# Sparse attention with a soft mixture of experts on one core: halving steps for the key chunks' minimum and maximum, the head product on GpSimd, and another order of the steps

## The chip, the core and the metric

The kernel runs on one core of a Trainium2 chip. A core has five engines that run side by side, each working through its own list of instructions in order: TensorE (PE in the profile; its weight loads are PEld), VectorE (DVE), ScalarE (ACT), GpSimd (POOL) and SyncE (SP). They wait for one another through semaphores. [...] Data comes from HBM through 16 DMA engines. In this kernel GpSimd issues all loads and SyncE issues all stores. The metric is the device time in microseconds, the median of three runs.

## What is computed

The first half is attention over chosen chunks of keys: 4 batches, 8 heads, 768 positions, head size 64. For each query and each chunk of 32 keys an upper bound of the score is made from the chunk's elementwise minimum and maximum, and the six best chunks (among those not in the future) take part in the attention.

```python
k_min = np.min(k_chunks, axis=3); k_max = np.max(k_chunks, axis=3)
ub = np.sum(np.maximum(q[:, :, :, None, :] * k_min[:, :, None, :, :],
                       q[:, :, :, None, :] * k_max[:, :, None, :, :]), axis=-1)
ub = np.where(causal, ub, -1e9)
top_chunks = np.argsort(ub, axis=-1)[..., -6:]
scores = np.where(sel & causal_mask, q @ k.T / 8, -1e9)
out = softmax(scores) @ v
```

The second half takes the 3072 rows of 512 that come out (x) through a soft mixture of 8 experts with 4 slots each: `logits = x @ phi`; a softmax down the rows gives each slot's input `d.T @ x`; each expert is `relu(slot @ w1) @ w2`; and a softmax over the slots spreads the results back to the rows, `c @ slot_out`.

## The kernel before

**Tiling.** Two heads make a pair, and 16 pairs (four to a batch) pass through a software pipeline: the loop at L469 runs over i, and one turn works on several pairs at once. It computes the scores of pair i, multiplies with the values for pair i-1, normalises and transposes the result of pair i-2, chooses chunks for pair i+1 and prepares keys and queries of pair i+2. "Pair i" in the text means turn i.

**Steps for a pair.** `load` (L122) issues the key and query loads on GpSimd's queue, four pairs ahead; `load_v` and `load_w` issue values and expert weights there too. `transposes` (L177) and `evac_T` (L189) bring keys and queries to SBUF as `kT` and `qT`, head size down the partitions, the copy on ScalarE. `kmin` and `kmax` (L199 to L213) reduce 24 chunks of 32 keys on VectorE into `mm`; then a product with `headsel` makes `bd`, in which each head's numbers stand in its own columns. `qsplit` (L215) splits queries into negative and positive part, `qpn`. `ubound` (L223) is 18 matmuls that make the bounds of all chunks, the causal term among them. `select` (L238) finds the eight largest per row with 12 instructions (`mx`), writes one column through a cast on GpSimd, and marks the chunks that are not chosen (`ns_t`). `ns_transposes` and `evac_ns` turn these marks into `nsT`. `scores(i, g)` (L264) makes one of six groups of score blocks: products of `kT` and `qT`, then a second pair of matmuls that add the mask from `nsT` and `smask`. `expo` (L283) is the exponential on ScalarE and, on GpSimd, the causal cut of the diagonal blocks. `pv` (L297) multiplies with the values. `normalise` (L313) divides (`inv`, `x_sb`), `x_transposes` and `evac_x` give `xT`.

**Steps for a batch.** When the last pair of a batch is through, the mixture's steps run inside the loop: `moe_logits`, `moe_copy` (`lg` and the row maximum `pm`), `moe_max` and `moe_bound` (the maximum over rows, `mb`), `moe_exp` (its spread `bc`, the running maximum `m_run`, the shifted logits `ld`, their exponential `d_sb`, the factor `dm`, and the rescaling of `si_acc`), `moe_comb` (`rm`, `lc`, and two exponentials into `c_pad`), `moe_dispatch` (`si_ps`) and `moe_ct` (`cT_all`). All of it falls in turn i-2 (logits and copy) and turn i-3 (the rest), counted from the batch's last pair. Batch 3 has its steps after the loop, before the experts.

**What sets the order.** The program is under a manual schedule: each engine gets its instructions in the order in which the Python code writes them. Nothing is moved by a planner. So a step that is written later on one engine waits behind everything that was written before it there.

**Buffers that tie engines together.** Score tiles come from `p_sc` with two buffers, so group g+2 needs the exponential of group g to be done. Transposes, bounds, marks and the mixture's small products share `p_tp` with two buffers (tag "tp"): each allocation needs the tile of the second allocation before it to have been read out. Exponentials are kept in nine buffers. Key and query inputs have three buffers each. Weights of the 16 expert matrices are loaded one a turn by a plan, in turns 2, 5, 8 and 11 none, in turns 12 and 13 two.

Of the kernel before, what the change touches and what calls it, by code (L numbers as in the profile page):

```python
# [46 lines left out]
def kernel(  # L47
# [61 lines left out]
    tpu = u_ctx.enter_context(tc.tile_pool(name="tpu", bufs=2, side="right"))  # L109
    inp = l_ctx.enter_context(tc.tile_pool(name="inp", bufs=3, side="right"))  # L110
# [87 lines left out]

    def kmin(i):  # L199
        kT = st["kT", i].rearrange("d (c x) -> d c x", x=CH)  # L200
        mm = tpu.tile([P, 2, 1, NCHUNK], BF16, name="mm", tag="mm")
        nc.vector.tensor_reduce(mm[:, 0, 0, :], kT, axis=AX.X, op=ALU.min)  # L202
        st["mm", i] = mm

    def kmax(i):
        kT = st["kT", i].rearrange("d (c x) -> d c x", x=CH)
        mm = st.pop(("mm", i))
        nc.vector.tensor_reduce(mm[:, 1, 0, :], kT, axis=AX.X, op=ALU.max)  # L208
        bd = tpu.tile([P, 2, 2, NCHUNK], BF16, name="bd", tag="bd")
        nc.vector.tensor_tensor(  # L210
# [144 lines left out]
    def moe_copy(b):  # L355
        lg = small.tile([P, NQT, NS], F32, name="lg", tag="lg")
        pm = small.tile([P, NS], F32, name="pm", tag="pm")
        ps = st.pop(("lgps", b))
        if b == B - 1:
            nc.vector.tensor_reduce(pm, ps.rearrange("p t s -> p s t"), axis=AX.X, op=ALU.max)  # L360
            nc.scalar.copy(lg, ps)
        else:
            nc.vector.tensor_copy(lg, ps)
            nc.vector.tensor_reduce(pm, lg.rearrange("p t s -> p s t"), axis=AX.X, op=ALU.max)
        st["lg", b], st["pm", b] = lg, pm
# [14 lines left out]
    def moe_exp(b):  # L380
        lg = st["lg", b]
# [3 lines left out]
        )  # L385
        m_new, m_old = m_run[b % 2], m_run[(b + 1) % 2]
# [51 lines left out]
    def moe_ct(b):  # L438
# [5 lines left out]
        nc.vector.tensor_copy(cT_all[:, b * NQT:(b + 1) * NQT, :], ps)  # L444
# [24 lines left out]
    for i in range(-2, NPAIR):  # L469
# [238 lines left out]
```

## Time and profile before

| | |
|---|---|
| median of three runs | 177.93 us (177.87 to 177.99) |
| the profiled execution's own time | 177.53 us |
| its span, first to last instruction | 175.8 us |
| TensorE, VectorE, ScalarE, GpSimd busy | 139.1, 128.8, 120.0, 99.9 us |
| first exponential of pairs 0, 1, 5, 9, 13 | 15.60, 23.48, 52.06, 82.47, 113.82 us |
| first exponential of pairs 14 and 15, end of the last one | 121.00, 130.21, 135.68 us |
| mean granted TensorE clock | 0.95 |

Times within the profile count from the first instruction. The profiled execution took 1.7 us more than its span, which lies around it. A busy share is an average over the start, the 16 turns and the tail (experts and output, from 144 us on), which have different limits. In a line of a timeline, the first number is the start, the second the time from the first to the last of the instructions merged into it, then engine, line, operation, the tile written and the tiles read, shapes and count; a bracket at the end gives the engine's idle time before it and what ended it. The lines of the changed kernel have other numbers, so groups are named by their tiles.

### The profile page before, as it was taken

What the parts mean: (1) busy time and instruction counts of PE and PEld (TensorE: products, weight loads), DVE (VectorE), ACT (ScalarE), POOL (GpSimd) and SP (SyncE); (2) the same over time, 40 slices, a digit from 0 to 9 for tenths busy, and PEclk for the clock granted to TensorE, in tenths of its full rate; (3) what the DMA queues carried; (4) which work ended last, traced back from release to release, by engine and by line L of the source; (5) the groups of instructions that cost most, each with busy time, mean ns of one, the idle gap of its engine ahead of it and who ended that gap; (6) DMA issues with size and microseconds to landing.
All of it is one profiled execution on the core that took longest, in us unless ns stands there. A gap on an engine that the chain in (4) does not pass through costs nothing.

```text
span 175.8 us, 5994 instructions
## 1 busy us (share of the span) xinstructions
PE 139.1 (79%) x2486; PEld 95.9 (55%) x2486; DVE 128.8 (73%) x429; ACT 120.0 (68%) x163; POOL 99.9 (57%) x194
## 2 busy tenths in 40 slices
PE   0449888999889889999988999999689569986500
PEld 0334556777567657766765776677467444532000
DVE  4456979999889998999998999999752650246530
ACT  2336798989789778988977698897667321156430
POOL 7995679869768557877775585759344600000000
PEclk9999999999999999999999999999999956999755
DMA  3999999999999999999999999199999993009995
GB/s 50 167 158 180 194 206 200 206 197 209 179 212 193 215 185 143 200 172 203 172 147 203 169 207 141 17 187 211 200 214 214 213 215 72 4 13 403 402 405 212
DMA packets 40460, 32.92 MB, mean 187 GB/s; under 512 B 26353, under 2 KB 34545, under 8 KB 40433
## 3 DMA queue, kind: packets, MB, share of 16 engines
q0 software_dynamic: 38416, 26.25, 101.8%
q1 hardware_dynamic: 2016, 6.29, 9.1%
q8 instruction: 19, 0.31, 0.7%
q14 instruction: 9, 0.07, 0.1%
HBM read 52.49 MB, written 6.29 MB: 334 GB/s over the span
## 4 chain that ended last, share of the span: by engine, by line
PE 36%; ACT 19%; DVE 13%; DMA 12%; POOL 11%; issue 5%; POOLq 0%; DVEq 0%; ACTq 0%
ACT e_sb L289 13%; DMA k_in<-in_k_dram 7%; PE sc_ps L271 6%; DMA out_dram<-o_sb 5%; PE at_ps L308 5%; PE sc_ps L277 4%; PE tr_ps L184 3%; PE h_ps L605 3%; DVE x_sb L321 3%; POOL e_sb L291 3%; POOL q_in L127 2%; PE ns_ps L253 2%; POOL k_in L127 2%; PE so_ps L640 2%; PE si_ps L427 2%
## 5 line engine op out<-in xcount | busy, mean ns | idle before, releaser
L289 ACT ACTIVATE e_sb<-sc_ps 128x1024 bf16<-128x1024 f32 x96 | 83.6, 936 | 10.9 <-PE sc_ps L277 9.9
L291 POOL TENSOR_SCALAR_AFFINE_SELECT e_sb<-e_sb 128x256 bf16<-128x256 bf16 x96 | 39.5, 423 | 32.7 <-ACT e_sb L289 32.0
L271 PE MATMUL sc_ps<-qT,kT 64*128 64x512 bf16 (+3 forms) x256 | 39.6, 310 | 6.6 <-ACT e_sb L289 6.3
L277 PE MATMUL sc_ps<-nsT,smask 64*128 64x512 bf16 (+3 forms) x256 | 36.8, 306 | 0.0
L308 PE MATMUL at_ps<-v_t,e_sb 128*128 128x65 bf16 x672 | 29.4, 194 | 1.2 <-DVE x_sb L321 1.1
L308 PEld LDWEIGHTS <-e_sb 128*128 128x128 bf16 x672 | 25.1, 98 | 3.4 <-DVE x_sb L321 1.6
L271 PEld LDWEIGHTS <-kT 64*128 64x128 bf16 x256 | 15.8, 94 | 16.8 <-issue 8.7
L242 DVE MAX8 mx<-ub_ps 128x8 f32<-128x24 f32 x192 | 18.8, 170 | 4.6 <-PE ub_ps L231 4.5
L202 DVE TENSOR_REDUCE mm<-kT 128x24 bf16<-128x768 bf16 x16 | 15.2, 949 | 4.0 <-ACT kT L193 4.0
L132 POOL DMA_DIRECT2D v_t<-in_v_dram x16 | 16.7, 1042 | 1.9 <-PE ns_ps L253 1.2
L193 ACT COPY kT<-tr_ps 128x768 bf16<-128x768 bf16 x16 | 12.8, 803 | 6.5 <-PE tr_ps L184 6.5
L321 DVE TENSOR_TENSOR x_sb<-at_ps,inv 128x768 bf16<-128x768 f32 (+2 forms) x17 | 15.5, 910 | 0.6
L277 PEld LDWEIGHTS <-smask 64*128 64x128 bf16 x256 | 13.1, 95 | 4.4 <-issue 0.3
L208 DVE TENSOR_REDUCE mm<-kT 128x24 bf16<-128x768 bf16 x16 | 15.1, 942 | 0.0
L193 ACT COPY qT<-tr_ps 128x768 bf16<-128x768 bf16 x16 | 13.2, 825 | 2.7 <-PE tr_ps L184 2.7
L184 PE MATMUL tr_ps<-ident,k_in 128*64 128x128 bf16 x192 | 9.2, 237 | 6.6 <-DMA k_in<-in_k_dram 5.5
L670 DVE TENSOR_SCALAR o_sb<-o_ps,cinv 128x512 f32<-128x512 f32 x12 | 8.6, 748 | 7.2 <-PE o_ps L668 4.1
L231 PE MATMUL ub_ps<-bd,qpn 128*128 128x48 bf16 x192 | 10.4, 187 | 2.8 <-DVE qpn L218 2.5
L127 POOL DMA_DIRECT2D k_in<-in_k_dram x16 | 11.7, 729 | 1.3 <-POOLq L692 0.8
L261 DVE COPY nsT<-ns_ps 128x768 bf16<-128x768 bf16 x16 | 8.9, 556 | 4.0 <-PE ns_ps L253 3.5
L672 ACT ACTIVATE o_sb<-o_ps,cinv 128x512 f32<-128x512 f32 x12 | 7.8, 688 | 5.7 <-DMA out_dram<-o_sb 3.8
L127 POOL DMA_DIRECT2D q_in<-in_q_dram x16 | 11.5, 721 | 0.0
(95 smaller groups left out, 213.2 us busy)
## 6 DMA issues: line engine op xcount, KB each, us to landing
w_sb<-in_moe_w_dram POOLq DMA_DIRECT2D x16, 1024.0 KB, 12.9
out_dram<-o_sb SPq DMA_DIRECT2D x10, 512.0 KB, 5.5
k_in<-in_k_dram POOLq DMA_DIRECT2D x16, 192.0 KB, 7.9
q_in<-in_q_dram POOLq DMA_DIRECT2D x16, 192.0 KB, 8.1
v_t<-in_v_dram POOLq DMA_DIRECT2D x16, 192.0 KB, 9.3
out_dram<-o_sb SPq DMA_DIRECT2D x4, 256.0 KB, 3.4
phi_sb<-in_moe_phi_dram POOLq DMA_DIRECT2D x1, 32.0 KB, 9.6
```

Of the source, the lines that this page charges most:

```text
L127: nc.gpsimd.dma_start(out=t, in_=src.rearrange("h (p g) d -> p h (g d)", p=P))
L132: nc.gpsimd.dma_start(out=v_t[i % NV][:, :, :, :D], in_=v[b, 2 * j:2 * j + 2].rearrange("h (g p) d -> p h g d", p=P),)
L193: nc.scalar.copy(t.rearrange("d (p g) -> d p g", g=NQT), st.pop((nm + "ps", i)).rearrange("d g p -> d p g"),)
L202: nc.vector.tensor_reduce(mm[:, 0, 0, :], kT, axis=AX.X, op=ALU.min)
L208: nc.vector.tensor_reduce(mm[:, 1, 0, :], kT, axis=AX.X, op=ALU.max)
L242: nc.vector.max(mx[:, a, :], ub[:, a, :])
L271: nc.tensor.matmul(ps[:, h, c:c + w], lhsT=kT[r, kg * P:(kg + 1) * P], rhs=qT[r, qs], start=True, stop=False,)
L277: nc.tensor.matmul(ps[:, h, c:c + w], lhsT=smask[r, kg].rearrange("p a b -> p (a b)"), rhs=nsT[r, qs], start=False, stop=True,)
L289: nc.scalar.activation(e[:, :, :w], st.pop(("scps", i, g))[:, :, :w], func=ACT.Exp, scale=scale)
L291: nc.gpsimd.affine_select(out=e[:, :, :P], in_=e[:, :, :P], compare_op=ALU.is_ge, fill=0.0, base=0, pattern=[[0, 2], [1, P]], channel_mult ...
L308: nc.tensor.matmul(o, lhsT=st["e", i, g][:, h, c:c + P], rhs=v_t[i % NV][:, h, kg, :], start=(kg == 0), stop=(kg == t),)
L321: nc.vector.tensor_tensor(st["x", b][:, t0:t1, 2 * j:2 * j + 2, :].rearrange("p t h d -> p h t d"), at[:, :, :, :D], inv.broadcast_to([P, ...
```

## The change

The change has two parts.

First, each of the two reductions over 32 keys becomes three steps, in a new function `fold`: the two halves of 16 keys are compared elementwise, then the two halves of 8 of the result, and what is left, 8 per chunk, is reduced. The intermediate tiles lie in a new pool `tpf` with one buffer each. The product that makes `bd` moves from VectorE to GpSimd.

Second, the order of the loop changes. `qsplit` goes from the end of the turn before to behind `normalise`. The bound and the selection go behind the key transposes and the first `pv` (in the first two turns they stay in front). The key and query loads follow the selection, as before. The query transposes and their copy go from before group 4 to between groups 4 and 5, and `kmax` with them. The mixture's functions are cut into smaller ones, and a batch's steps now spread over the turns i-2 (logits), i-3 (copy, maximum, bound, the shifted logits for the combine weights, spread), i-4 (shift, exponential, rescale, weights, dispatch, the transposes of the weights) and i-5 (their copy out). After the loop the steps of batch 3 have the same order as before; the copy of batch 2's transposed weights falls there too, on ScalarE.

```diff
+    tpf = u_ctx.enter_context(tc.tile_pool(name="tpf", bufs=1, side="right"))
...
+    def fold(out, kT, op):
+        a = tpf.tile([P, NCHUNK, CH // 2], BF16, name="fold_a", tag="fold_a")
+        nc.vector.tensor_tensor(a, kT[:, :, :CH // 2], kT[:, :, CH // 2:], op=op)
+        b = tpf.tile([P, NCHUNK, CH // 4], BF16, name="fold_b", tag="fold_b")
+        nc.vector.tensor_tensor(b, a[:, :, :CH // 4], a[:, :, CH // 4:], op=op)
+        nc.vector.tensor_reduce(out, b, axis=AX.X, op=op)
+
     def kmin(i):
...
-        nc.vector.tensor_reduce(mm[:, 0, 0, :], kT, axis=AX.X, op=ALU.min)
+        fold(mm[:, 0, 0, :], kT, ALU.min)
...
     def kmax(i):
...
-        nc.vector.tensor_reduce(mm[:, 1, 0, :], kT, axis=AX.X, op=ALU.max)
+        fold(mm[:, 1, 0, :], kT, ALU.max)
         bd = tpu.tile([P, 2, 2, NCHUNK], BF16, name="bd", tag="bd")
-        nc.vector.tensor_tensor(
+        nc.gpsimd.tensor_tensor(
             bd, mm.broadcast_to([P, 2, 2, NCHUNK]), headsel.broadcast_to([P, 2, 2, NCHUNK]), op=ALU.mult,
         )
...
-        moe(moe_max, i - 3)
-        if have(i + 1):
-            ubound(i + 1)
         if have(i - 2):
             normalise(i - 2)
-        moe(moe_bound, i - 3)
+        moe(moe_copy, i - 3)
+        moe(moe_shift, i - 4)
+        moe(moe_exp, i - 4)
+        moe(evac_ct, i - 5)
         if have(i + 1):
+            qsplit(i + 1)
+        if i <= 0 and have(i + 1):
+            ubound(i + 1)
             select(i + 1)
         if have(i + 2):
             transposes(i + 2, "k")
             evac_T(i + 2, "k")
+        if have(i - 1):
+            pv(i - 1, [0, 1, 2])
+        if i > 0 and have(i + 1):
+            ubound(i + 1)
+            select(i + 1)
         if i == -1:
             ns_transposes(0)
             evac_ns(0)
         if have(i + 4) and i >= -1:
             load(i + 4, "k")
             load(i + 4, "q")
-        if have(i - 1):
-            pv(i - 1, [0, 1, 2])
-        moe(moe_exp, i - 3)
+        moe(moe_top, i - 3)
+        moe(moe_rescale, i - 4)
         if have(i):
             scores(i, 2)
             expo(i, 2)
             scores(i, 3)
             expo(i, 3)
+        moe(moe_weights, i - 4)
         if have(i - 2):
             x_transposes(i - 2)
         if have(i - 1):
             pv(i - 1, [3])
         if have(i + 2):
-            transposes(i + 2, "q")
-            evac_T(i + 2, "q")
             kmin(i + 2)
         if have(i - 2):
             evac_x(i - 2)
-        if have(i + 2):
-            kmax(i + 2)
-        moe(moe_comb, i - 3)
         if have(i + 2) and i >= 0:
             load_v(i + 2)
         if i < EARLY:
             weights(i)
         if have(i):
             scores(i, 4)
             expo(i, 4)
+        moe(moe_max, i - 3)
+        moe(moe_dispatch, i - 4)
+        if have(i + 2):
+            transposes(i + 2, "q")
+            evac_T(i + 2, "q")
+        moe(moe_bound, i - 3)
+        if have(i + 2):
+            kmax(i + 2)
+        moe(moe_comb, i - 3)
+        if have(i):
             scores(i, 5)
             expo(i, 5)
         if have(i + 1) and i >= 0:
             ns_transposes(i + 1)
             evac_ns(i + 1)
         if have(i - 1):
             pv(i - 1, [4])
-        moe(moe_dispatch, i - 3)
-        if have(i - 1):
             pv(i - 1, [5])
-        if have(i + 2):
-            qsplit(i + 2)
...
-        moe(moe_ct, i - 3)
+        moe(moe_spread, i - 3)
+        moe(moe_ct, i - 4)
         moe(moe_logits, i - 2)
-        moe(moe_copy, i - 2)
...
+    evac_ct(B - 2, nc.scalar.copy)
     normalise(LAST - 1)
...
-    moe_copy(B - 1)
+    moe_top(B - 1)
+    moe_copy(B - 1, nc.scalar.copy)
     moe_max(B - 1)
     moe_bound(B - 1)
+    moe_spread(B - 1)
+    moe_shift(B - 1)
     moe_exp(B - 1)
+    moe_comb(B - 1)
+    moe_weights(B - 1)
+    moe_rescale(B - 1)
     moe_dispatch(B - 1)
```

The functions that the loop calls by new names hold the old instructions: `moe_copy` the copy `lg`, `moe_top` the maximum `pm`; `moe_spread` the matmul `bc`, `moe_shift` the steps `m_run`, `ld` and `dm`, `moe_exp` the two exponentials, `moe_rescale` the product on `si_acc`; `moe_comb` the steps `rm` and `lc`, `moe_weights` the two exponentials into `c_pad`; `moe_ct` the transposes and `evac_ct` their copy.

More of the change, by code (lines that the diff above doesn't have):

```diff
@@ L353, in moe_logits, with moe_copy, moe_top @@
                 )
-    def moe_copy(b):
+    def moe_copy(b, copy=nc.vector.tensor_copy):
         lg = small.tile([P, NQT, NS], F32, name="lg", tag="lg")
+        copy(lg, st["lgps", b])
+        st["lg", b] = lg
+    def moe_top(b):
         pm = small.tile([P, NS], F32, name="pm", tag="pm")
[L358 to L365, printed above, removed]
+        src = st["lgps", b] if b == B - 1 else st["lg", b]
+        nc.vector.tensor_reduce(pm, src.rearrange("p t s -> p s t"), axis=AX.X, op=ALU.max)
+        st["pm", b] = pm
     def moe_max(b):
@@ L378, in moe_bound, with moe_spread @@
         st["mb", b] = mb
-    def moe_exp(b):
-        lg = st["lg", b]
+    def moe_spread(b):
         bc = p_tp.tile([P, NS], F32, name="bc_ps", tag="tp")
@@ L385, in moe_exp, with moe_shift @@
         )
+        st["bc", b] = bc
+    def moe_shift(b):
+        lg, bc = st["lg", b], st.pop(("bc", b))
         m_new, m_old = m_run[b % 2], m_run[(b + 1) % 2]
@@ L394, in moe_exp @@
         )
-        d_sb = small.tile([P, NQT, NS], BF16, name="d_sb", tag="d_sb")
-        nc.scalar.activation(d_sb, ld, func=ACT.Exp)
-        st["d", b] = d_sb
+        st["ld", b] = ld
         if b > 0:
@@ L401, in moe_exp, with moe_rescale @@
             nc.vector.tensor_tensor(dm[:, 0, :], m_old, m_new, op=ALU.subtract)
+            st["dm", b] = dm
+    def moe_exp(b):
+        d_sb = small.tile([P, NQT, NS], BF16, name="d_sb", tag="d_sb")
+        nc.scalar.activation(d_sb, st.pop(("ld", b)), func=ACT.Exp)
+        st["d", b] = d_sb
+        if b > 0:
+            dm = st["dm", b]
             nc.scalar.activation(dm, dm, func=ACT.Exp)
-            if b == B - 1:
-                moe_comb(b)
+    def moe_rescale(b):
+        if b > 0:
+            dm = st.pop(("dm", b))
             nc.vector.tensor_tensor(si_acc, si_acc, dm.broadcast_to([P, NDG + 1, NS]), op=ALU.mult)
     def moe_comb(b):
-        lg = st.pop(("lg", b))
+        lg = st["lg", b]
         rm = small.tile([P, NQT, 1], F32, name="rm", tag="rm")
@@ L413, in moe_comb, with moe_weights @@
         nc.vector.tensor_tensor(lc, lg, rm.broadcast_to([P, NQT, NS]), op=ALU.subtract)
+        st["lc", b] = lc
+    def moe_weights(b):
+        lc = st.pop(("lc", b))
         for g in range(2):
@@ L443, in moe_ct, with evac_ct @@
             )
-        nc.vector.tensor_copy(cT_all[:, b * NQT:(b + 1) * NQT, :], ps)
+        st["ctps", b] = ps
+    def evac_ct(b, copy=nc.vector.tensor_copy):
+        copy(cT_all[:, b * NQT:(b + 1) * NQT, :], st.pop(("ctps", b)))
     def have(i):
@@ L592 @@
     moe_ct(B - 1)
+    evac_ct(B - 1)
     cinv = tail.tile([P, B * NQT], F32, name="cinv")
```

## The prediction

> **What bounds the kernel now.** I read the busy table first, then a table by stage, then the timelines of a plain pair (one without the mixture steps), last the start. The busy table: no engine is full.
>
> ```profile
> PE 139.1 (79%) x2486; PEld 95.9 (55%) x2486; DVE 128.8 (73%) x429; ACT 120.0 (68%) x163; POOL 99.9 (57%) x194
> ```
>
> The stretches (us, then busy us of PE, PEld, DVE, ACT, POOL, then clock, DMA share, GB/s) are pairs 9 to 12 (one whole batch period), 14 and 15. TensorE is within 2.2 us of full in the batch period and VectorE within 2.3; pair 14 has idle time on every engine.
>
> ```profile
> 82.47:113.82 31.35, 29.12 (x579) 21.54 (x575) 29.06 (x100) 26.49 (x37) 20.67 (x41) 1.00 1.14 153
> 121.00:130.21 9.21, 7.37 (x147) 5.51 (x143) 6.67 (x28) 5.78 (x10) 5.05 (x12) 1.00 1.25 205
> 130.21:135.68 5.47, 4.31 (x83) 3.15 (x80) 1.62 (x4) 5.07 (x6) 1.83 (x5) 1.00 1.06 213
> ```
>
> Pair 8, VectorE's timeline (start, us, what, in brackets the idle time before):
>
> ```profile
> 76.61 1.17 DVE L242 MAX8 mx<-ub_ps 128x8 f32<-128x24 f32 x12 [0.24 <-PE ub_ps L231]
> 77.82 0.46 DVE L245 TENSOR_TENSOR ns_t<-ub_ps,mx 128x288 bf16<-128x288 f32 x1
> 78.28 0.95 DVE L202 TENSOR_REDUCE mm<-kT 128x24 bf16<-128x768 bf16 x1
> 79.15 0.55 DVE L341 COPY xT_sb<-xT_ps 128x768 bf16<-128x768 bf16 x1
> 79.61 0.94 DVE L208 TENSOR_REDUCE mm<-kT 128x24 bf16<-128x768 bf16 x1
> 80.59 0.26 DVE L210 TENSOR_TENSOR bd<-mm,headsel 128x96 bf16<-128x96 bf16 x1
> 80.91 0.56 DVE L261 COPY nsT<-ns_ps 128x768 bf16<-128x768 bf16 x1
> 81.38 0.44 DVE L218 TENSOR_SCALAR qpn<-qT 128x768 bf16<-128x768 bf16 x1
> 81.75 0.34 DVE L219 TENSOR_SCALAR qpn<-qT 128x768 bf16<-128x768 bf16 x1
> 82.01 0.22 DVE L320 RECIPROCAL inv<-at_ps 128x12 f32<-128x12 f32 x1
> 82.26 0.96 DVE L321 TENSOR_TENSOR x_sb<-at_ps,inv 128x768 bf16<-128x768 f32 x1
> ```
>
> Only 0.24 of the 6.85 us is idle: `qpn` was made a pair early, so the bound's matmuls run while VectorE normalises. The pair is closed by the handover of a score buffer, in the timelines of TensorE and ScalarE:
>
> ```profile
> 74.91 0.39 PE L271 MATMUL sc_ps<-qT,kT 64*128 64x512 bf16 x2 [0.19 <-ACT e_sb L289]
> ```
> ```profile
> 75.61 1.94 ACT L289 ACTIVATE e_sb<-sc_ps 128x1024 bf16<-128x1024 f32 x2 [0.48 <-PE sc_ps L277]
> ```
>
> The start, GpSimd's and VectorE's timelines, and the chain in pair 4, where a key load pins the transposes to 45.8 us:
>
> ```profile
> 9.32 2.07 POOL L132 DMA_DIRECT2D v_t<-in_v_dram  x2
> 12.46 0.29 POOL masks.py:199 TENSOR_SCALAR_AFFINE_SELECT identf<-identf 128x128 f32<-128x128 f32 x1
> 12.71 0.23 POOL L244 CAST ns_t<-mx 128x12 bf16<-128x12 f32 x1
> ```
> ```profile
> 10.50 1.17 DVE L242 MAX8 mx<-ub_ps 128x8 f32<-128x24 f32 x12 [0.92 <-PE ub_ps L231]
> ```
> ```profile
> 33.22 12.54 DMA k_in<-in_k_dram
> ```
>
> The sum below is against the profiled execution: span 175.8, own time 177.53. The median of the three runs, 177.93, is 0.40 above it, which I add at the end. Within 0.2% (0.36 us) a measurement can't tell from no change.
>
> **The fold.** A reduction over 768 goes (0.95); two elementwise steps with 384 and 192 results and a reduction over 192 come. Fixed part: 0.95 - 768/0.96 GHz = 0.15, and the same from `bd` (0.26 - 0.10). No row has an elementwise bf16 step on two SBUF inputs at full rate. The nearest is the bf16 copy, 0.56, which moves 2 a cycle (0.15 + 0.40); ends are 1 a cycle (`bd`) and 4 (`qpn`, 0.35). At 2: 0.35 + 0.25, the reduction over 192 as `rm` of the same size, 0.35, and 0.035 twice because each step needs the one before (gap of `ns_t` after `mx`): 1.02, so 0.07 more than before. Ends: 0.87 and 1.32. The halving does fewer passes but pays the fixed part three times. With `bd` gone (0.26 + 0.03), VectorE gains only 0.15 a pair.
>
> [...]
>
> [...]
>
> In the trace `bd` took 0.26 in 14 of 16 cases and 0.65 and 0.39 in two, with selects on GpSimd beside it: 0.033 each on average. Four such steps a pair give 0.13, of which I put 0.1 on the path.
>
> **`bd` on GpSimd.** Between the row for 12 elements (0.23) and twice that of the 128-element select (0.33, one input, so 0.66): 0.35, nearer the smaller size. It stands behind the select of group 4. In pairs that load weights GpSimd's queue runs cast 0.23, loads 1.44, two selects 0.83, value load 1.02, weight load 0.70, select 0.4, `bd`. The loads follow the selection, which comes 0.9 later in the pair than now, so `bd` ends 1.9 us into the next pair, just when `qpn` is ready there. Covered by that; the far end costs 0.3 in 8 pairs. SP's queue issues nothing here.
>
> **The plain pair.** T=0 is the start of its first scores. `pv` of the last pair ends there, `inv` starts at 0.2, `x_sb` ends at 1.4, the two `qpn` at 1.95 (0.27 each after overlap). Now the bound's matmuls come right behind: TensorE has scores, key transposes and `pv` till 1.9, then waits for `qpn`. From the matmuls' start to `mx` is 0.69 (75.92 to 76.61), so VectorE idles 0.7 in place of 0.24. `mx` 2.65, `ns_t` ends 4.3, the first fold 5.3, `xT` 5.8. `ns_transposes` needs the PSUM slot that `xT` frees (two slots, the second allocation before it): TensorE, there at 5.5, waits till 5.8, takes 0.35 and 0.85 for `pv`: 7.05. VectorE's second fold and `nsT` end at 7.1. So the loop closes at 7.05, with the 0.1 above 7.15, against 6.85. The handover wait does go, since the query copy moves between the last two exponentials: ScalarE needs only 6.4. But it was not the only bound.
>
> **The batch, over three pairs.** Same durations. Logits pair: TensorE ends 0.65 later, `lg` hides there: 7.55. Next pair: `lg`, `pm` 0.4, `mb` 0.2, `rm` and `lc` 0.7, the shift 0.65, all on VectorE in front of the next bound: 8.75. Third: rescale 0.3, sum 0.3, `cT` 0.5: 8.35 (8.0 in batch 0, which has no rescale). Fourth: 7.05. Sum 31.7 (31.4 in batch 0), plus 0.5 for 0.1 each and two more folds in the long pair: 32.2 and 31.9, against 31.35 and 30.41. The stalls of the old long pair (10.27 for 9.28 of VectorE) go, but the idle 0.7 before `mx` now comes in all four.
>
> **Pair 14 and the end.** Pair 14 has no fold and no key or query step, and its shift, dispatch and rescale move to pair 15: TensorE and VectorE in turn give 6.6, against 9.21. Pair 15 gains an exponential, two weights steps (0.9 on ScalarE) and 1.1 of matmuls; its last `pv` ends 0.3 later than now. The extra ScalarE copy of `cT` lies in its 1.8 us wait after the loop. The rest of the tail has the same order. Weight loads move with the pairs: the page's DMA row falls to 3 in its slice from 145 to 149 us, and the last eight weights are read from 150.2 on, so 3 us of lag between the two stay hidden.
>
> **The start.** `bd` of pair 0 now waits on GpSimd behind two value loads, `phi` and `identf`: 12.75 to 13.1, where VectorE had it at 8.7. Bound (0.8, slow clock), `mx` from 14.05 to 15.2, cast 15.25, against 12.71: the first exponential comes 2.5 late. Pair 0 gives back 0.3: pair 1 begins at 25.7 (23.48 before). Pair 1 has nothing to normalise: 6.7. Three pairs at 7.15 make 53.85 for pair 5, against 52.06; the 0.95 wait of pair 4 for its key load is covered by the delay. Net +1.8.
>
> **Sum:** 1.8 + 1.5 (batch 0) + 0.85 (batch 1) + 0.45 (pair 13: 7.65 for 7.18) - 2.6 + 0.3 = +2.3. 177.53 + 2.3 + 0.4 = 180.2.
>
> **Rivals.**
> - *TensorE closes every pair (faster).* If the loop from `pv` to `pv` comes under TensorE's own 6.64, pairs cost what TensorE is busy: batches 28.7 and 29.1 (-1.7, -2.2), pair 13 even, pair 14 -2.6, end +0.3, start +0.3 after three short pairs: -5.9, 172.0. For it: the scores' handover wait goes. Against: it needs 0.4 off the loop, more than the whole range of one fold allows (0.15).
> - *Only small prices.* Folds run at 4 a cycle, no contention, `bd` of pair 0 hurts less: -2 to -3 on my sum, 177 to 178. Against: the start's queue is in the trace.
> - *The fold runs at 1 a cycle, or GpSimd blocks it.* 0.3 each, one and most of the other on the loop, 0.4 in 13 pairs: +5, 185. For it: `bd` runs so; against: its inputs repeat elements, the fold's don't.
>
> **Numbers.** Forecast 0.52, TensorE-bound 0.13, small prices 0.18 (0.10 faster, 0.08 the same), unpacked 0.17. Faster 0.23, same 0.08, slower 0.69. The range drops the fastest case and the far part of the last: 175 to 185.3; for the forecast alone 178.4 to 182.5.
>
> **What would show it.** Right: `mx` behind an idle 0.6 to 0.8 in plain pairs with the bound's matmuls waiting for `qpn`; a period near 7.1; fold steps near 0.35, 0.25, 0.35; the first exponential near 18; pair 14 under 7. Wrong: plain pairs at 6.7 or less with TensorE unbroken, or a first step of 0.55.

## The result and the profile after

The changed kernel takes 182.38 us (median of four runs, 181.67 to 183.16) against 177.9 (176.21 to 177.99): a ratio of 1.030, with a 95% interval of 1.026 to 1.033, or 4.5 us by the medians and some 5 us by the ratio. The forecast had the direction and a part of the mechanism, the idle time in front of `mx`; the loss is about twice the forecast one (177.9 to 180.2). The profiled execution took 182.43 us (span 180.7), 4.90 more than that of before.

The busy table of the changed kernel:

```profile
PE 140.3 (78%) x2486; PEld 96.5 (53%) x2486; DVE 124.4 (69%) x476; ACT 121.0 (67%) x164; POOL 107.1 (59%) x210
```

VectorE has 4.4 us less work than before (128.8), GpSimd 7.2 more (99.9), and yet the kernel is slower. So the busy sums do not explain the loss; the place of the work and the waits have to. Two lines of the table of waits (engine, tile, who was waited for: us in total, times, longest):

```profile
DVE mx L250 <- PE ub_ps L239: 14.6, 14, 4.8
...
PE ub_ps L239 <- POOL bd L218: 7.0, 3, 5.9
```

In the costliest groups of before, VectorE's idle time in front of `mx` was 4.6 us in all; here it is 17.6. And TensorE now waits for `bd`, of which the waits of before had no line; 5.9 of the 7.0 is the first such wait, in the start.

The table by stage of the changed kernel (stretch in us, its length, then busy us of PE, PEld, DVE, ACT, POOL, clock, DMA share, GB/s): turns 0 to 4, pairs 5 to 8, pairs 9 to 12, 13, 14 and 15.

```profile
18.55:25.87 7.32, 5.91 (x80) 3.29 (x77) 5.64 (x26) 6.47 (x8) 4.81 (x10) 1.00 1.25 207
25.87:32.78 6.91, 6.58 (x126) 4.63 (x125) 5.32 (x24) 6.47 (x9) 5.31 (x12) 1.00 1.39 200
32.78:41.04 8.26, 6.84 (x132) 4.87 (x128) 6.24 (x26) 6.46 (x9) 7.33 (x15) 1.00 1.33 201
41.04:48.49 7.45, 6.72 (x132) 4.91 (x128) 6.44 (x26) 6.37 (x8) 5.73 (x12) 1.00 1.33 170
48.49:56.02 7.53, 6.86 (x132) 4.84 (x128) 6.52 (x26) 6.47 (x9) 6.10 (x12) 1.00 1.25 181
56.02:88.17 32.15, 29.40 (x579) 21.69 (x575) 28.03 (x110) 26.49 (x35) 24.27 (x49) 1.00 1.26 176
88.17:120.43 32.26, 29.23 (x579) 21.73 (x575) 28.00 (x112) 26.59 (x37) 22.84 (x45) 1.00 1.06 137
120.43:128.28 7.85, 7.38 (x156) 5.45 (x152) 6.84 (x27) 6.46 (x8) 6.30 (x13) 1.00 1.25 199
128.28:135.21 6.93, 6.51 (x111) 4.58 (x107) 5.97 (x25) 5.07 (x6) 5.05 (x12) 1.00 1.32 205
135.21:140.88 5.67, 5.17 (x108) 3.80 (x105) 2.05 (x7) 5.67 (x10) 1.86 (x6) 1.00 1.06 214
```

Against the same stages of before, by the first exponentials of the pairs:

| stage | before | after | difference | forecast |
|---|---|---|---|---|
| to the first exponential of pair 0 | 15.60 | 18.55 | +2.95 | +2.5 |
| turns 0 to 4 | 36.46 | 37.47 | +1.01 | -0.7 |
| pairs 5 to 8 | 30.41 | 32.15 | +1.74 | +1.5 |
| pairs 9 to 12 | 31.35 | 32.26 | +0.91 | +0.85 |
| pair 13 | 7.18 | 7.85 | +0.67 | +0.45 |
| pair 14 | 9.21 | 6.93 | -2.28 | -2.6 |
| the rest (pair 15, tail, time around the span) | 47.32 | 47.22 | -0.10 | +0.3 |
| profiled execution | 177.53 | 182.43 | +4.90 | +2.3 |

From pair 5 on every stage lies within 0.4 us of the forecast. Of the 2.6 us that the forecast lacks, 2.2 arose before pair 5's first exponential: 0.45 in the start, 1.1 in turn 2, 0.7 in turns 3 and 4 (all three forecast at 7.15), while turns 0 and 1 nearly cancel.

From one selection of the changed kernel to the next (turns 2 and 3), VectorE's timeline:

```profile
36.87 0.46 DVE L253 TENSOR_TENSOR ns_t<-ub_ps,mx 128x288 bf16<-128x288 f32 x1
37.24 0.35 DVE L202 TENSOR_TENSOR fold_a<-kT 128x384 bf16<-128x384 bf16 x1
37.62 0.26 DVE L204 TENSOR_TENSOR fold_b<-fold_a 128x192 bf16<-128x192 bf16 x1
37.98 0.35 DVE L205 TENSOR_REDUCE mm<-fold_b 128x24 bf16<-128x192 bf16 x1
38.25 0.55 DVE L349 COPY xT_sb<-xT_ps 128x768 bf16<-128x768 bf16 x1
38.72 0.55 DVE L202 TENSOR_TENSOR fold_a<-kT 128x384 bf16<-128x384 bf16 x1
39.30 0.34 DVE L204 TENSOR_TENSOR fold_b<-fold_a 128x192 bf16<-128x192 bf16 x1
39.68 0.35 DVE L205 TENSOR_REDUCE mm<-fold_b 128x24 bf16<-128x192 bf16 x1
...
41.81 0.35 DVE L227 TENSOR_SCALAR qpn<-qT 128x768 bf16<-128x768 bf16 x1
42.90 0.19 DVE L250 MAX8 mx<-ub_ps 128x8 f32<-128x24 f32 x1 [0.74 <-PE ub_ps L239]
```

Two things are to be seen. VectorE stands idle for 0.74 us between `qpn` and `mx`, while TensorE makes the bounds, as the forecast said (0.7). And the same fold takes 1.10 us (37.24 to 38.34) the first time and 1.31 (38.72 to 40.03) the second. GpSimd's timeline says what lay beside them, a key load's issue beside the first, two selects and a value load's issue beside the second:

```profile
37.13 0.77 POOL L128 DMA_DIRECT2D k_in<-in_k_dram  x1
...
38.62 0.91 POOL L299 TENSOR_SCALAR_AFFINE_SELECT e_sb<-e_sb 128x256 bf16<-128x256 bf16 x2
39.49 1.02 POOL L133 DMA_DIRECT2D v_t<-in_v_dram  x1
```

The turn of pair 2, the longest of the early ones, TensorE's and GpSimd's timelines:

```profile
34.97 0.21 PE L239 MATMUL ub_ps<-bd,qpn 128*128 128x48 bf16 x2 [0.89 <-POOL bd L218]
```
```profile
30.24 0.77 POOL L128 DMA_DIRECT2D k_in<-in_k_dram  x1 [0.63 <-PE sc_ps L285]
31.00 0.72 POOL L128 DMA_DIRECT2D q_in<-in_q_dram  x1
31.73 0.78 POOL L299 TENSOR_SCALAR_AFFINE_SELECT e_sb<-e_sb 128x256 bf16<-128x256 bf16 x2
32.45 1.02 POOL L133 DMA_DIRECT2D v_t<-in_v_dram  x1
33.47 0.71 POOL L121 DMA_DIRECT2D w_sb<-in_moe_w_dram  x1
34.18 0.43 POOL L299 TENSOR_SCALAR_AFFINE_SELECT e_sb<-e_sb 128x256 bf16<-128x256 bf16 x1
34.55 0.36 POOL L218 TENSOR_TENSOR bd<-mm,headsel 128x96 bf16<-128x96 bf16 x1
```

`mm` was complete at 31.77 and `qpn` at 33.91; `bd` ends at 34.91, since GpSimd comes to it only behind the seven other instructions shown. TensorE stands for 0.9 us in the middle of the bound.

### The profile page after: what moved, and what is told of

It reads as the page before. It is cut to its first block, busy times and chain, and to the rows that moved or that the text cites. A ratio compares the mean times of both kernels' runs of the same rounds, so it can differ in the third digit from the quotient of the medians.

```text
span 180.7 us, 6078 instructions
## 1 busy us (share of the span) xinstructions
PE 140.3 (78%) x2486; PEld 96.5 (53%) x2486; DVE 124.4 (69%) x476; ACT 121.0 (67%) x164; POOL 107.1 (59%) x210
## 4 chain that ended last, share of the span: by engine, by line
DVE 39%; PE 31%; POOL 9%; ACT 7%; DMA 4%; issue 4%; DVEq 0%; POOLq 0%; ACTq 0%
DVE mx L250 9%; PE at_ps L316 5%; DMA out_dram<-o_sb 4%; DVE mm L205 4%; ACT e_sb L297 4%; PE ub_ps L239 4%; DVE fold_a L202 4%; DVE fold_b L204 4%; PE sc_ps L279 3%; DVE ns_t L253 3%; DVE x_sb L329 3%; DVE xT_sb L349 3%; PE h_ps L647 3%; PE sc_ps L285 3%; PE tr_ps L185 3%
## 5 line engine op out<-in xcount | busy, mean ns | idle before, releaser
L299 POOL TENSOR_SCALAR_AFFINE_SELECT e_sb<-e_sb 128x256 bf16<-128x256 bf16 x96 | 40.9, 439 | 16.7 <-ACT e_sb L297 16.2
L250 DVE MAX8 mx<-ub_ps 128x8 f32<-128x24 f32 x192 | 18.8, 172 | 17.6 <-PE ub_ps L239 14.6
L279 PEld LDWEIGHTS <-kT 64*128 64x128 bf16 x256 | 14.8, 94 | 11.5 <-issue 3.7
L239 PE MATMUL ub_ps<-bd,qpn 128*128 128x48 bf16 x192 | 11.7, 188 | 8.5 <-POOL bd L218 7.0
L285 PEld LDWEIGHTS <-smask 64*128 64x128 bf16 x256 | 13.9, 95 | 7.4 <-issue 3.2
L202 DVE TENSOR_TENSOR fold_a<-kT 128x384 bf16<-128x384 bf16 x32 | 12.8, 399 | 3.8 <-ACT kT L194 3.8
L239 PEld LDWEIGHTS <-qpn 128*128 128x128 bf16 x192 | 9.4, 98 | 10.3 <-issue 5.2
L128 POOL DMA_DIRECT2D k_in<-in_k_dram x16 | 12.3, 766 | 1.9 <-POOLq L734 0.8
L252 POOL CAST ns_t<-mx 128x12 bf16<-128x12 f32 x16 | 3.7, 234 | 16.3 <-DVE mx L250 16.3
L205 DVE TENSOR_REDUCE mm<-fold_b 128x24 bf16<-128x192 bf16 x32 | 11.3, 353 | 2.1
L185 PEld LDWEIGHTS <-k_in 128*64 128x64 bf16 x192 | 6.3, 116 | 10.5 <-issue 5.5
```

The lines of the kernel that those rows point to most:

```text
L185: nc.tensor.matmul(ps[h * 64:(h + 1) * 64, g, :], lhsT=src[:, h, g * D:(g + 1) * D], rhs=ident, is_transpose=True,)
L202: nc.vector.tensor_tensor(a, kT[:, :, :CH // 2], kT[:, :, CH // 2:], op=op)
L205: nc.vector.tensor_reduce(out, b, axis=AX.X, op=op)
L239: nc.tensor.matmul(ps[:, t, :], lhsT=qpn[:, x, t * P:(t + 1) * P], rhs=bd[:, x].rearrange("p h c -> p (h c)"), start=False, stop=(x == 1),)
L250: nc.vector.max(mx[:, a, :], ub[:, a, :])
L279: nc.tensor.matmul(ps[:, h, c:c + w], lhsT=kT[r, kg * P:(kg + 1) * P], rhs=qT[r, qs], start=True, stop=False,)
```

## The experiments

All ratios are to the kernel before, run on the same chip beside them; its medians were 177.9 us beside the changed kernel and 176.88 to 177.29 beside the others. Two theories stood at the outset. A: VectorE's loop through the bound, with its idle time in front of `mx`, closes the turn, and `bd` on GpSimd costs the start and the turns of pairs 1 and 2. B: the order itself gains, and the halving steps, stretched by GpSimd, are the loss. The expectations of the later runs name their own A and B.

| run | ratio (95% interval) | median us |
|---|---|---|
| changed kernel | 1.030 (1.026 to 1.033) | 182.38 |
| order_alone | 1.002 (0.999 to 1.006) | 177.65 |
| steps_alone | 1.011 (1.007 to 1.016) | 179.04 |
| bd_on_vector | 1.039 (1.034 to 1.043) | 183.99 |
| early_bound | 1.010 (1.005 to 1.015) | 178.65 |
| start_on_vector | 1.014 (1.007 to 1.022) | 179.30 |
| spread_alone | 0.985 (0.979 to 0.991) | 174.65 |
| fold_alone | 1.004 (1.001 to 1.008) | 178.15 |
| no_selects | 1.003 (0.999 to 1.006) | 177.41 |
| issues_behind | 1.031 (1.026 to 1.035) | 182.78 |
| bound_late | 1.021 (1.018 to 1.024) | 181.06 |
| evac_first | 0.983 (0.980 to 0.986) | 174.43 |
| evac_first_bd | 0.982 (0.978 to 0.986) | 174.40 |

### The order without the halving steps, and the steps without the order

`order_alone` is the changed kernel with the plain reductions, and the head product on VectorE:

```diff
-        fold(mm[:, 0, 0, :], kT, ALU.min)
+        nc.vector.tensor_reduce(mm[:, 0, 0, :], kT, axis=AX.X, op=ALU.min)
...
-        nc.gpsimd.tensor_tensor(
+        nc.vector.tensor_tensor(
             bd, mm.broadcast_to([P, 2, 2, NCHUNK]), headsel.broadcast_to([P, 2, 2, NCHUNK]), op=ALU.mult,
```

> The new order with the two reductions over 32 keys and the head product on VectorE, as before the change. Theory A (VectorE's idle time in front of mx closes the turn, and the product on GpSimd costs the start and pairs 1 and 2): first exponential at 16.0 us, no late bd in pair 2, but mx still idles 0.7 us behind the bound's matmuls, plain pairs at 7.2 (7.2 to 7.5 in the changed kernel); total 177.5 to 179. Theory B (the loss is the halving steps, stretched by GpSimd, and the order itself gains): plain pairs near 6.7, total 171 to 174.

`steps_alone` is the kernel before with `fold` and with the head product on GpSimd, in the old order.

> The old order with the halving steps and the head product on GpSimd. Theory A: the start is 2.5 us late as in the changed kernel, 0.95 of it taken up by pair 4's wait for its key load; in the turns the two folds (1.1 to 1.2 us each) cost VectorE what the moved product saves, plain pairs 6.85 to 7.0; total 179 to 180.5. Theory B (halving is what costs): plain pairs over 7.1, total 181.5 or more. If halving frees VectorE as its fewer elements say: 173 to 176.

Both came out as theory A had them. `order_alone` is level with before: plain turns are 7.05 to 7.2 (6.85 before; that of pair 2 7.84), the two batch periods 31.43 and 31.71 (30.41 and 31.35), and pair 14 gives 2.3 back (6.88 for 9.21). `steps_alone` loses 1.1%, in the start: the first exponential of pair 0 comes at 18.40, that of pair 1 at 26.70 (15.60 and 23.48), while the plain turns stay at 6.85. But the two losses, 0.2% and 1.1%, do not add up to 3.0%. The steps cost 1.1% in the old order and 2.7% (1.030 less 1.002) in the new one. So B falls in so far as it saw a gain in the whole order; the stretch of the halving steps that it named is still open here.

### The head product back on VectorE

`bd_on_vector` is the changed kernel with the product on VectorE, halving steps and order kept (the last two lines of the diff above).

> The changed kernel with only the head product put back on VectorE. Theory A: first exponential back at 16.0 us, pair 2 from 8.26 to 7.5, but 0.3 us more on VectorE in each of 13 turns that it closes; total 180 to 182. Theory B (GpSimd's product is what stretches the halving steps): the steps keep 0.35 and 0.26 us throughout and the total falls to 177 to 178.

Neither number was met. The start is restored (first exponential at 15.69), yet the kernel is slower than the changed one: the turns of pairs 3, 6, 8, 10 and 12 are 0.5 to 0.8 us longer (pairs 5 to 8 together: 33.7 us by the first exponentials, against 32.15). Its groups on VectorE (mean ns after the busy us):

```profile
L202 DVE TENSOR_TENSOR fold_a<-kT 128x384 bf16<-128x384 bf16 x32 | 13.2, 412 | 3.7 <-ACT kT L194 3.7
L205 DVE TENSOR_REDUCE mm<-fold_b 128x24 bf16<-128x192 bf16 x32 | 11.3, 353 | 1.1
L204 DVE TENSOR_TENSOR fold_b<-fold_a 128x192 bf16<-128x192 bf16 x32 | 9.9, 310 | 1.1
L218 DVE TENSOR_TENSOR bd<-mm,headsel 128x96 bf16<-128x96 bf16 x16 | 5.1, 321 | 0.6
```

A fold takes 0.412 + 0.310 + 0.353 and two gaps of 0.035, so 1.145, where the reduction it replaces took 0.945 in the run of the order alone: 0.20 more, 32 times, makes 6.4 us. The two runs differ by 1.0385 - 1.0024 = 3.6%, 6.4 us. So as a sum the new order pays for the folds in full. Turn by turn it is uneven: against `order_alone` turns 3, 6, 8, 10 and 12 are 0.7 to 1.0 us longer, turn 0 is 0.7 longer, and the others at most 0.3.

### The product of the first two pairs alone

`start_on_vector` is the changed kernel with

```diff
-        nc.gpsimd.tensor_tensor(
+        (nc.vector if i <= 1 else nc.gpsimd).tensor_tensor(
             bd, mm.broadcast_to([P, 2, 2, NCHUNK]), headsel.broadcast_to([P, 2, 2, NCHUNK]), op=ALU.mult,
```

> The changed kernel, with the head product of pairs 0 and 1 alone on VectorE. It prices the wait for GpSimd's queue in the start. Theory A (the late product of pairs 0 and 1 is a loss of its own that nothing later hides): first exponential of pair 0 at 15.6 to 16.0 in place of 18.55, time 182.4 less 2.0 to 2.8: 179.6 to 180.4. Rival B (the later pairs wait for their key loads, so that an earlier start is given back, as 0.7 of it was in the run with the steps alone): gain of 0 to 1.0: 181.4 to 182.4. Pair 2's turn (8.26) must stay in both, since its product is still on GpSimd for pair 2 and its queue is late there by an issue of a key load.

A held: the ratio falls by 1.5% of before, 2.7 us, and the median by 3.1, a little more than A's 2.8; the first exponential is back at 15.66 and pair 2's turn stays long (8.04). In the single profiles the gain is smaller, 1.55 us at the end of the last exponential, as turn 0 took 8.99 here and 7.32 in the changed kernel; the last section says why such a difference need not belong to the kernels. Beside `bd_on_vector` the run also gives the price of the product where it is not in the start: with pairs 2 to 15 on GpSimd the ratio is 2.4% lower, 4.3 us, and 14 times the product's 0.321 is 4.5. So over the later turns together the move to GpSimd is worth about all of VectorE's time for it, and its cost lies in the first two pairs; turn 2 (8.04 here, 7.74 in `bd_on_vector`) is an exception.

### The halving steps alone

`fold_alone` is the kernel before with `fold`, the product on VectorE, the old order.

> The kernel before, with the halving steps alone: order as before, head product on VectorE. Together with the run of both steps it parts the fold from the head product on GpSimd. Theory A (each fold costs 0.07 to 0.25 more than the reduction it replaces, VectorE is 96% full in a plain pair of the old order): plain turns 7.0 to 7.2 in place of 6.85, start unchanged at 15.6, time 179.5 to 182. Rival B (the fold is hidden in the old order and the start is the whole loss of the steps alone): 177.5 to 178.5.

The median lies in B's range: 0.44%, 0.8 us. A's turns did not come: the plain ones stay at 6.85, although a fold takes as long as in the new order (0.410 and 0.293 for the two halving steps). The old order's plain turn had 0.24 of idle time on VectorE and was closed by the handover of a score buffer; there the folds hide. In the profile turns 6 and 10 pay (9.98 and 11.74 for 9.51 and 10.27) and turn 0 is longer (8.72 for 7.88); the last exponential ends 1.9 us later, of which the tail gives 1.1 back. The rest of what `steps_alone` lost is, by difference, the product on GpSimd in the start.

### The selects taken away

`no_selects` leaves out the causal cut inside the diagonal blocks:

```diff
-        nc.gpsimd.affine_select(
-            out=e[:, :, :P], in_=e[:, :, :P], compare_op=ALU.is_ge, fill=0.0,
-            base=0, pattern=[[0, 2], [1, P]], channel_multiplier=-1,
-        )
```

> The changed kernel without GpSimd's selects on the exponentials (the causal mask inside the diagonal blocks is left out, so the weights of later keys stay in). It shows what the selects beside VectorE's halving steps cost. Theory A (contention: the first halving step takes 0.50 beside a select and 0.35 without): all halving steps at 0.35 and 0.26 but those beside a DMA issue, turns of plain pairs 7.05 to 7.2 in place of 7.45 to 7.55, time 178 to 180. Rival B (the steps are slow for another reason, and the turns are closed by the bound's waits): the means stay near 0.40 and 0.30, the plain turns within 0.1 of 7.45, time 181.5 to 182.5 (less what an emptier GpSimd queue gives in pairs 0 to 2, about 1).

This is the run that settles the miss. The halving steps without selects on GpSimd, and then those of the changed kernel (mean ns after the busy us):

```profile
L202 DVE TENSOR_TENSOR fold_a<-kT 128x384 bf16<-128x384 bf16 x32 | 11.2, 349 | 3.8 <-ACT kT L194 3.7
L204 DVE TENSOR_TENSOR fold_b<-fold_a 128x192 bf16<-128x192 bf16 x32 | 8.3, 258 | 1.1
```
```profile
L202 DVE TENSOR_TENSOR fold_a<-kT 128x384 bf16<-128x384 bf16 x32 | 12.8, 399 | 3.8 <-ACT kT L194 3.8
...
L204 DVE TENSOR_TENSOR fold_b<-fold_a 128x192 bf16<-128x192 bf16 x32 | 9.6, 301 | 1.1
```

The reduction of 192 takes 353 ns in both. Turns 2, 3 and 4 without the selects:

```profile
33.34:40.41 7.07, 6.72 (x132) 4.86 (x128) 6.06 (x26) 6.37 (x9) 3.84 (x7) 1.00 1.38 202
40.41:47.37 6.96, 6.61 (x132) 4.91 (x128) 5.95 (x26) 6.37 (x9) 3.51 (x6) 1.00 1.36 179
47.37:54.33 6.96, 6.61 (x132) 4.97 (x128) 5.94 (x26) 6.46 (x8) 3.67 (x6) 1.00 1.33 199
```

They sum to 20.99 against 23.24 with the selects; the forecast's loop without contention was 7.05 a turn, 21.15. So what the forecast lacked in these turns, 1.79 us (23.24 less three times 7.15), is gone with the selects.

In turn 3 VectorE's loop can be followed step by step. From `mx` to `mx` it takes 7.73 us in the changed kernel (42.90 to 50.63) and 6.96 without the selects (42.27 to 49.23). Four of the changed kernel's steps make 0.76 of the 0.77 between them, the halving steps of the second fold (0.55 and 0.55 for 0.35 and 0.26) and the query splits (0.42 and 0.55 for 0.35 each):

```profile
45.96 0.55 DVE L202 TENSOR_TENSOR fold_a<-kT 128x384 bf16<-128x384 bf16 x1
46.54 0.55 DVE L204 TENSOR_TENSOR fold_b<-fold_a 128x192 bf16<-128x192 bf16 x1
...
49.00 0.42 DVE L226 TENSOR_SCALAR qpn<-qT 128x768 bf16<-128x768 bf16 x1
49.34 0.55 DVE L227 TENSOR_SCALAR qpn<-qT 128x768 bf16<-128x768 bf16 x1
```

A rival is that the load issues on GpSimd stretch the halving steps. But in `no_selects` 59 of the 64 halving steps run beside a load issue alone, and none of these takes over 0.36 (first step) or 0.26 (second).

In all the run gains 2.7%, 4.8 us, more than A said (down to 178), because it takes away at least three things at once: the stretch of the halving steps, that of the query splits (`qpn` 0.371 and 0.355, in the changed kernel 0.481 and 0.393), and the delay of `bd` in GpSimd's queue. What each of them is worth in the whole time is not parted.

The contention of VectorE's steps with the selects is thereby shown, and with it the half of the first theory B that was open: the first halving step took 0.55 beside two selects and 0.35 alone.

### Load issues behind the product

`issues_behind` is the changed kernel with `load_v` and `weights` moved from before group 4 to behind `kmax`, so that `bd` stands ahead of them on GpSimd's queue.

```diff
+        if have(i + 2):
+            kmax(i + 2)
+        if have(i + 2) and i >= 0:
+            load_v(i + 2)
+        if i < EARLY:
+            weights(i)
```

> The changed kernel, with the value and weight load of a turn issued on GpSimd's queue behind the head product in place of ahead of it. Theory A (in the turns of pairs 1 and 2 the bound waits for the head product because GpSimd's queue holds it behind load issues of 0.7 to 1.0): the waits of the bound for the product go, the turn of pair 2 falls from 8.26 to 7.4 to 7.6, time 181.0 to 181.7. Rival B (what is late is GpSimd as such, and the issues now hold up the selects of the next pair): turn of pair 2 over 8.0 or others longer by as much, time 182 to 183.

The bound's wait for the product in turn 2 goes, as A has it, but the time is B's. Turn 2 falls from 8.26 to 7.75 only (with the product on VectorE, in `order_alone`, it took 7.84), because the next thing is late: the value load's issue now lies beside the query splits, without a select (the second takes 0.88 and ends at 34.12), and the bound waits 0.38 for it.

```profile
34.17 0.20 PE L239 MATMUL ub_ps<-bd,qpn 128*128 128x48 bf16 x1 [0.38 <-DVE qpn L227]
```

Turn 8 grows from 7.40 to 7.96, and the last exponential ends at 140.88 as in the changed kernel. One wait was traded for another: in the changed kernel GpSimd was busy for 7.33 of turn 2's 8.26 us, more than a plain turn should last, so whatever stands last in its queue is late.

### Where the order gains and where it loses

`spread_alone` is the kernel before with the mixture steps alone spread as the change has them; bound, query split, query copy, reductions and product stay as before.

> The kernel before, with the mixture steps alone spread over three pairs as the change has them; the bound stays a pair early in its place in front of the normalisation, the query copy, the plain reductions and the head product stay as they were. Theory A (the order of the mixture steps gains, the moved bound with its idle time in front of mx loses): plain turns stay at 6.85, the batches come to 30.0 and 30.4 (30.41 and 31.35 before), pair 14 falls from 9.2 to under 7: 3 to 4.5 in all, 173.5 to 175.0. Rival B (the long turns are as long as VectorE's work, however it is spread, and the order alone gained nothing because of that): 177 to 178.5.

A, within its range: 174.65, 1.5% faster than before. One of its terms was wrong: pairs 5 to 8 take 31.20 (30.41 before, 30.0 expected); pairs 9 to 12 take 30.47 (31.35, and 30.4 expected). The two batch periods together are level with before (61.67 against 61.76), so in the profile the gain is pair 14's (the third line here; the first is a plain turn, the second pairs 5 to 8):

```profile
38.07:44.92 6.85, 6.63 (x132) 4.85 (x128) 6.44 (x23) 6.37 (x8) 5.25 (x11) 1.00 1.26 201
52.02:83.22 31.20, 29.00 (x579) 21.36 (x575) 29.50 (x100) 26.56 (x36) 23.15 (x45) 1.00 1.35 198
...
120.88:127.26 6.38, 6.20 (x111) 4.26 (x107) 5.50 (x23) 5.14 (x6) 4.83 (x12) 1.00 1.32 204
```

`bound_late` is `order_alone` with the query copy back in its old place, so `spread_alone` with the bound and the selection behind the value products; the query split, `kmax` and the small steps `mb`, `rm` and `lc` stand where the change has them too.

> The run with the new order alone, with the query transposes and the query copy back in front of the copies of groups 4 and 5. So it is the spread mixture order with the bound behind the value products, and with the queries split a turn later; beside the run with the spread alone it prices the moved bound, beside the run of the new order alone the late query copy. Theory A (the bound behind the value products, with its idle time in front of mx, loses the 3.0 between those two runs): plain turns 7.05 to 7.2, time 177 to 178.5. Rival B (the late query copy loses it): plain turns 6.85, time 174.3 to 175.5.

Slower than both theories allowed: 181.06. Against `spread_alone` (0.985) the late bound, with what moves along, costs 3.6%, 6.4 us: 0.2 in a plain turn (7.01 for 6.85) and 2.5 to 3.2 in a batch period (33.7 and 33.6, first exponentials). The late query copy then gives back 1.9%, 3.3 us (1.021 to 1.002); in the profiles 2.3 and 1.9 of it lie in the two batch periods. So the direction of A holds and its size does not: the two groups of edits have opposite signs, and only their sum is the 3.1 us that the first runs showed. A part of what the early query copy costs under a late bound can be read; it needs the slot of the bound, which the late selection frees late (`order_alone` has no such line among its longer waits):

```profile
PE tr_ps L185 <- DVE ns_t L253: 3.0, 12, 0.3
```

`early_bound` is `order_alone` with the bound right behind groups 0 and 1, `qsplit` at the end of the turn before, the selection ahead of the first value products, and these ahead of the key transposes.

```diff
+        if have(i + 1):
+            ubound(i + 1)
         if have(i - 2):
             normalise(i - 2)
...
+        if have(i + 2):
+            qsplit(i + 2)
```

> The new order of the mixture's steps and of the query copy, with reductions and head product on VectorE, but qsplit again at the end of the turn before and the bound's matmuls right behind the first scores; pv goes ahead of the key transposes. Theory A: mx follows x_sb with at most 0.3 us idle, TensorE closes the plain pairs at 6.6 to 6.8, pairs with mixture steps 7.2 to 8.2, total 170 to 174, below both kernels. Theory B (the spread over three turns or the late query copy costs in itself): total 177 or more.

A's 170 to 174 was missed by far, and the time, 178.65, is in B's range. The waits show two faults of the edit. The value products wait for the normalisation, which frees their only PSUM tile, and the key transposes, now behind them, wait along with them; and `qsplit`, in front of the normalisation, waits for the late query copy. The table of waits, then VectorE's timeline (the reciprocal of the normalisation follows the two splits at 84.74):

```profile
ACT kT L194 <- PE tr_ps L185: 9.9, 12, 3.7
...
PE at_ps L316 <- DVE x_sb L329: 4.7, 10, 0.6
```
```profile
83.74 0.60 DVE L226 TENSOR_SCALAR qpn<-qT 128x768 bf16<-128x768 bf16 x1 [0.18 <-ACT qT L194]
```

So, as these waits read, an early bound and a late query copy do not go together: the copy's delay passes through the split into the normalisation and the value products. No run takes the two faults out one by one. They belong to this build and say nothing against an early bound as such, which `spread_alone` has.

### Towards a better kernel

`evac_first` is `spread_alone` with the logits copy, the shift and the copy of `cT` ahead of the normalisation:

```diff
-        if have(i - 2):
-            normalise(i - 2)
         moe(moe_copy, i - 3)
         moe(moe_shift, i - 4)
         moe(moe_exp, i - 4)
         moe(evac_ct, i - 5)
+        if have(i - 2):
+            normalise(i - 2)
```

> The run with the mixture steps spread alone, with the three mixture evacuations of a turn's start (logits copy, shift, cT copy) ahead of the normalisation in place of behind it. There the key transposes wait for them, since they free the PSUM slot (0.6 to 1.0 in the three long turns of a batch period). Theory A (that wait is on the path): the long turns lose 0.3 to 0.5 each, 172.0 to 173.7. Rival B (VectorE's work closes these turns, and the value products now wait for the later normalisation instead): 174.2 to 175.0.

`evac_first_bd` moves the product of pairs 2 and later to GpSimd on top.

> The run evac_first, with the head product of pairs 2 and later on GpSimd. Theory A (the product is made half a turn before the early bound reads it, so GpSimd's queue hides it and VectorE gains 0.29 where it closes the turn, in the long turns): plain turns 6.85, long turns 0.2 to 0.3 shorter, 0.5 to 1.5 below evac_first. Rival B (GpSimd is late with it and the early bound waits): equal to evac_first or up to 1 above it.

Both are level with `spread_alone` within the intervals (174.43 and 174.40 against 174.65). For `evac_first` that is B's number, but the sum of its batch periods is shorter (30.42 and 30.25 against 31.20 and 30.47); whether a part of A is real is not settled by it. For the product, B. The three runs are the kernels that beat both: 1.5 to 1.8% faster than before, 4.3 to 4.7% faster than the changed one.

## Why the prediction was right and wrong

The ratios form a ladder in which each rung is one edit or one group of edits (percent of the time before, each to 0.6 to 0.9, and us). A rung's price holds only on top of the rungs above it: the folds cost 0.8 us in the old order and 6.4 here.

| rung | change |
|---|---|
| mixture steps spread (spread_alone) | -1.5%, -2.6 us |
| bound and selection behind the value products, with later split, `kmax` and query copy (order_alone) | +1.7%, +3.1 us |
| halving steps (bd_on_vector) | +3.6%, +6.4 us |
| product of pairs 2 to 15 on GpSimd (start_on_vector) | -2.4%, -4.3 us |
| product of pairs 0 and 1 on GpSimd (the changed kernel) | +1.5%, +2.7 us |

**The plain pair: right in mechanism.** "VectorE idles 0.7 in place of 0.24" measured 0.74, and the bound's matmuls start when `qpn` is there: in turn 3 the first that reads it starts at 42.18, where the second split ends at 42.16. TensorE came there at the same moment, so in this turn it hardly waited. The loop of 7.05 without contention measured 6.96 to 7.07 in `no_selects`, and 7.05 to 7.2 in `order_alone`.

**The contention: the first step that failed.** "Four such steps a pair give 0.13, of which I put 0.1 on the path" was sized by `bd`, a short step that a select had met in two of 16 cases. The halving steps meet one far more often (8 of the 32 first steps take 0.44 to 0.62 beside a select): on average they lose 0.050 and 0.043 (399 less 349, 301 less 258), so 0.19 a pair for the four, and the query splits another 0.15. Turns 3 and 4 measured 7.45 and 7.53 for 7.15: 0.30 and 0.38 more than forecast, 0.49 and 0.57 more than without the selects. The fold itself was priced right: 1.02 forecast, 0.35 + 0.26 + 0.35 and two gaps measured where nothing lies beside it. The "0.96 GHz" and the fixed part of 0.15 in it stand for what rows of before show: `x_sb` takes 957 ns for 768 results and 423 for 256, so 1.04 ns a result (0.96 in a nanosecond, "1 a cycle" in the forecast's words) and 0.156 us besides. By the same count the copy into `xT_sb` makes about two in that time (549 ns for 768, 292 for 256) and `qpn` about four (0.35 us for 768).

```profile
L321 DVE TENSOR_TENSOR x_sb<-at_ps,inv 128x768 bf16<-128x768 f32 x15 | 14.4, 957 | 0.5
...
L321 DVE TENSOR_TENSOR x_sb<-at_ps,inv 128x256 bf16<-128x256 f32 x1 | 0.4, 423 | 0.0
```

**The product on GpSimd: half right, and the second step that failed.** The start was read from the right queue: 2.5 late was forecast, 2.95 measured, and the price in the times is 2.7. "`bd` ends 1.9 us into the next pair, just when `qpn` is ready there. Covered by that" failed in the turns of pairs 1 and 2. There `bd` ended 0.6 and 1.0 after `qpn` (27.32 and 34.91 against 26.75 and 33.91), for GpSimd was late there. In turn 1 TensorE came to the bound at 27.3 anyway; in turn 2 it stood for 0.89. Turn 2 took 8.26 for the forecast 7.15, the largest single error. The sum had nothing for this; the far end beside it, 0.3 in 8 pairs, had neither the size nor the place. Not all of turn 2's 1.1 is the product's: with the product on VectorE the turn still takes 7.74 (`bd_on_vector`) and 7.84 (`order_alone`). In `order_alone` the second query split, beside selects, takes 0.91 where it takes 0.35 a turn later, and the bound waits 0.64 for it:

```profile
31.85 0.91 DVE L227 TENSOR_SCALAR qpn<-qT 128x768 bf16<-128x768 bf16 x1
```

So 0.4 to 0.5 of the 1.1 goes with the product; the rest stays in both of these runs, which keep the selects, and is gone in `no_selects` (7.07). The product's time was right (0.35 forecast, 0.34 to 0.48 measured).

**The batches, pairs 13 and 14, the end: right as sums.** No term is off by more than 0.4: 32.15 and 32.26 for 31.9 and 32.2, 7.85 for 7.65, 6.93 for 6.6, and the end 0.4 better. Without the selects the two batch periods take 31.28 and 31.60, against 31.4 and 31.7 forecast without contention. So the selects cost 0.87 and 0.66 there, some 0.2 a turn where 0.1 was forecast; the 2.25 of turns 2 to 4 (23.24 less 20.99) are the exception. The four turns of the first period, counted from `mx` to `mx`, took 7.50, 9.05, 8.09 and 7.23 for 7.55, 8.75, 8.0 and 7.05 before the 0.1 each. Two of the forecast's turns do not follow from the terms listed with them: 7.05 and 1.95 make 9.0, not 8.75, and 7.05 and 1.1 make 8.15, not 8.35; the two slips nearly cancel.

**The rivals.** TensorE closing every pair did not come: its plain turns were never under 6.9. Nor did the small prices, 177 to 178. The unpacked fold, 185, is out as a mechanism, since without the selects the steps took 0.35 and 0.26, which the forecast had worked out for two a cycle (0.35 and 0.25); its other half, that GpSimd blocks the fold, is what took the result to that side of the forecast.

## What to carry to other kernels

Before a reduction is replaced by shorter steps, ask who runs beside them: the price of a VectorE step must be read beside the GpSimd work that it will meet (a halving step of 0.35 us took 0.44 to 0.62 beside a select here), not from a step that seldom met it. A gain in an engine's busy time counts where that engine's loop closes the turn and not elsewhere: the same folds cost 0.8 us in one order and 6.4 in the other. Moving a short step to an in-order queue full of load issues pays where the queue is early (4.3 us here, over 14 pairs) and costs its backlog where it is late (2.7 us for the first two), so look at the first turns one by one. And a change of many parts should be taken apart: here one part, the spread of the mixture steps, was worth 1.5%, nearly all of it in pair 14, and the rest buried it.

## What was not expected of the hardware

In these profiles TensorE's matmuls take longer for a while at the start, and when that ends differs from one to the next. `evac_first` and `evac_first_bd` are the same up to pair 2's product, which GpSimd comes to at 21.7 us. Their transposes of the same keys on TensorE's timeline, first the one, then the other:

```profile
17.91 0.85 PE L185 MATMUL tr_ps<-ident,k_in 128*64 128x128 bf16 x12
```
```profile
17.65 0.53 PE L185 MATMUL tr_ps<-ident,k_in 128*64 128x128 bf16 x12
```

Twelve transposes take 0.85 us in the slow phase and 0.53 after it, while the profile's granted clock reads 1.00 in both stretches, so that column does not show the phase. The forecast's "slow clock" beside pair 0's bound is this phase: in the changed kernel these matmuls took 0.83 us there (13.28 to 14.11) and 0.62 in turn 3 (42.18 to 42.80), at a granted clock of 1.00 both times. Over all fourteen profiles turn 0 took 7.07 to 7.90 us in the six where the transposes were fast by 20.7 us, and 8.14 to 8.99 in the eight where they were not. The changed kernel's profile was among the first six, that of `start_on_vector` among the others, which fits that these two show less difference than the times do. The slow phase ends at 16 to 25 us, long after TensorE's first matmuls at 4.7 to 5.1; what ends it is not shown.
